# Sections of 12 tiles with one and two units of values in turn, and a last stretch of score pairs and whole products

## The chip, the cores and the metric

The kernel runs on one core of a Trainium2 chip. Its time is the device time of one execution in microseconds; the number compared is the median of several runs. Engines are named as in the profile: PE (TensorE), DVE (VectorE), ACT (ScalarE), POOL (GpSimd) and SP (the queue that issues most DMAs).

## What is computed

There are two branches over 2048 tokens of width 512, mixed by a gate for each token:

```python
a = x @ hid_re.T;  b = x @ hid_im.T            # 2048 x 512 each
y = seq_re @ a - seq_im @ b                    # a DFT of 2048 over the tokens, real part
q, k, v = split(xb @ wqkv)                     # 32 heads of 16
o = softmax(q @ k.T * 16**-0.5) @ v            # full attention, 2048 x 2048 for each head
g = sigmoid((x * gate_w).sum(-1))
out = g * y + (1 - g) * (o @ wo)
```

Everything is fp32. The weights of the attention are large, so the softmax needs each row's true maximum.

## The kernel before

**First stage** (to about 265 us of the span). The projections of x and xb are computed as sums of three products of high and low parts in fp32r (lines 78 to 80), and q and k go to DRAM.

**Main stage.** Two heads make a pair p, one in rows 0 to 63 of the array ("half 0"), one in rows 64 to 127 ("half 1"); products on different halves run at the same time. A pair has 32 *units* u: 2 halves of the queries (1024 each) by 16 blocks of 128 keys, so there are 512 units. Four kinds of work are interleaved:

- *a tile* (`a_tile`, line 196): a 128 x 512 block of scores in one of the three PSUM banks of `psA`, whose row maxima DVE takes (line 203). When 64 of them have closed half a pair, DVE reduces the maxima (`nm`, line 207), and `m_rows` (line 211) transposes them on PE into another `psA` bank, splits them on DVE and writes them by DMA into rows of `qs`, so that the scores come out with the maximum subtracted. The a tiles run 42 ahead of the units' need.
- *score* (`scores`, line 554), "s": keys by queries, 128 x 512, in one of the three banks of `psS`; ACT takes the exp into `pt` (line 564). A unit has four: two blocks of queries by two heads.
- *values* (`pv`, line 566): eight products of a unit on PE into the bank `acc`, in four column groups (line 572). After 16 units ACT copies `acc` out (line 576), and only then may the next unit write there.
- *DFT products* ("d", line 316): 32 chains of 48 products, each chain accumulating in the only bank of `psD`. Each product has 128 rows and is issued as two half products. A list of them is run first on half 0 while a tiles and scores run on half 1 beside it, then the same list on half 1 with tiles on half 0. Products on different halves may not write one bank together, so the first list product of a section waits for the reader (DVE or ACT) of a tile that was issued after the last one of the section before; line 726 adds that wait. At the end of a chain ACT or DVE reads the bank (lines 345, 348).

The order is written out by hand as patterns. Each token of a pattern is a slot: a single letter is one list product beside one tile on the other half; two letters are two tiles, one on each half, and no list product; a bar is one unit of values.

```python
FULL = "a s a s a s s a s a s a s a s a | |"
THIN = "aS s s a a s a | a s a a s s sA |"
```

FULL segments take lists of 16, and THIN segments lists of 12, so a chain takes three pairs of FULL or four pairs of THIN; the chains take turns (`pairs`, line 735). A segment holds two units. `pairs` goes on with eight THIN pairs over lists of 9 of the output product (`proj(1, (0, 1, 2))`), one chain for each list, read by DVE in `finish` (line 456).

**Last 30 units** (`weave`, line 613). Two units' scores with lists of 9 of the remaining output products, in half products, with a drain of PE ahead of each half (`turn`), then two units of values. Part of the scores use banks of `psA`. `last_pair` (line 494) turns the last sums by PE transposes, divides, multiplies by the last rows of wo and writes out.

**Plan.** `at(u, f)` runs a step ahead of unit u's section: `sums` loads the softmax sums from DRAM, `inverse` takes reciprocals on DVE (line 397), `block` and `last_block` load, multiply and split a block of the attention's output, and `load_yg` brings back the DFT result. `load_stacks` loads a pair's q and k.

Of the kernel before, what the change touches and what calls it, by code (L numbers as in the profile page):

```python
# [9 lines left out]
F32 = mybir.dt.float32  # L10
# [5 lines left out]
P = 128  # L16
S = 2048
D = 512
H = 32
DH = 16  # L20
NP = H // 2
KT = D // P
NT = S // P
UNITS = NP * 32
# [7 lines left out]
def mix_kernel(ctx: ExitStack, tc: tile.TileContext, xa_t, xa, wqkv, w_hid, w_seq, wo, gate_w, out):  # L32
# [5 lines left out]
    nc = tc.nc  # L38
# [142 lines left out]
    def load_stacks(p):  # L181
        q_t, k_t = qs[p % 2], ks[p % 2]
        for h in range(2):
            rows = slice((2 * p + h) * DH, (2 * p + h + 1) * DH)
            o = 64 * h

            for i, (qv, kv) in enumerate(((0, 0), (0, 1), (1, 0))):
                part = slice(o + 16 * i, o + 16 * i + 16)
                nc.sync.dma_start(q_t[part].bitcast(F32), qk_d[0][qv, rows])
                nc.sync.dma_start(k_t[part].bitcast(F32), qk_d[1][kv, rows])  # L190
# [33 lines left out]
    def run_deferred():  # L224
        while deferred:
            m_rows(*deferred.pop(0))
# [12 lines left out]
    a_next = 0  # L239
# [218 lines left out]
    def proj(hf, cts, pools):  # L458

        for qt in range(8):  # L460
            t = hf * 8 + qt
            chain = Chain(*pools[qt % len(pools)], 3 * len(cts))
            for ct in cts:
                h1, l1 = oh[hf, ct][qt]
                for i, (st, mv) in enumerate(((h1, 0), (h1, 1), (l1, 0))):
                    last = ct == cts[-1] and i == 2
                    yield chain, st, wos[0][:, mv, ct], partial(proj_next, hf, cts, t, chain) if last else None
# [6 lines left out]
    def load_yg(hf, ts):  # L474
        if hf:
            for t in ts:
                yp[t] = work.tile([P, D], F32, name=f"yp{t}", tag=("craw", "ch", "cl")[t % 3], bufs=3)
        else:
            for i, x in enumerate(("qs0", "ks0")):
                y4 = main.tile([P, 4, D], F32, name=f"yp_{x}", tag=x)  # L480
                yp.update({4 * i + k: y4[:, k] for k in range(4)})
        for t in ts:
            nc.sync.dma_start(yp[t], yg_d[t])

# [66 lines left out]

    pts = {}

    def scores(u, qb, h):
        p, r = divmod(u, 32)
        hf, kt = divmod(r, 16)
        q0 = hf * 1024 + qb * 512
        if u not in pts:
            pts[u] = work.tile([P, 4, 512], F32, name="pt", bufs=4)
        spare = a_next >= NP * 64 and qb and u < 500  # L560
        ps = psA.tile([P, 512], F32, name="a") if spare else psS.tile([P, 512], F32, name="s")
        rr = slice(64 * h, 64 * h + 50)
        nc.tensor.matmul(ps, ks[p % 2][rr, kt * P:(kt + 1) * P], qs[p % 2][rr, q0:q0 + 512], start=True, stop=True)  # L563
        return nc.scalar.activation(pts[u][:, 2 * qb + h], ps, AF.Exp, bias=0.0, scale=DH ** -0.5)  # L564
# [15 lines left out]
    def take(gen, n, whole=True):  # L580

        got = []
        while len(got) < n:
            x = next(gen, None)
            if x is None:
                break
            x[0].left -= 1
            got.append((*x, x[0].left == 0))
            if whole and got[-1][4]:
                break  # L590
        return got

    def issue(x, half, stop=True):
        chain, st, mv, after, last = x
        i = chain.mm(st, mv, half, last and stop)
        if stop and after:
            after()
        return i

    def turn():  # L600

        nc.tensor.drain()

    def pump(gen, n):
        for x in take(gen, n):
            issue(x, None)

    def drain(gen):
        while xs := take(gen, 9):
            for x in xs:  # L610
                issue(x, None)

    def weave(q, ds):

        m = len(q[0]) - 1
        n = min(len(ds), m)
        if ds:
            turn()
        for i in range(n):
            q[0][i]()  # L620
            issue(ds[i], 1, False)
        for x in ds[n:]:
            issue(x, 1, False)
        for i in range(n, m + 1):
            q[0][i]()
            q[1][i - n]()
        rest = q[1][m + 1 - n:]
        if ds:
            turn()
        for i, x in enumerate(ds):  # L630
            issue(x, 0)
            if i < len(rest):
                rest[i]()

    fill = iter(())
    plan = {2: [gate]}

    def at(u, f, *args):
        plan.setdefault(u, []).append(partial(f, *args))
# [9 lines left out]
                    for step, du in enumerate((16, 20, 22)):  # L649
                        at(last + du + 8 * half, block, step, hf, ct, half)  # L650

    def start(gen, n, whole=True):
        nonlocal fill, rate
        drain(fill)
        fill, rate = gen, (n, whole)

    one, more = [(psD, "d")], [(psD, "d"), (psA, "a"), (psA, "a")]
    at(482, start, proj(0, (0, 1, 2), one), 9)
    at(482, load_yg, 0, range(8))
    for step, u in enumerate((490, 494, 496)):  # L660
        at(u, last_block, step, 1, 3, nc.gpsimd)
    at(500, start, proj(1, (3,), more), 9, False)
    for step, u in enumerate((500, 502, 504)):
        at(u, last_block, step, 0, 4, nc.vector)
    at(506, start, proj(0, (3,), more), 9, False)
    at(500, load_w15)
    rate = (7, True)
    lead = a_next

    def ahead(k):  # L670
        return min(lead + 4 * k, NP * 64)

    def queue(k, h):

        q = []
        for i in range(4):
            q.append(partial(scores, 2 * k + i // 2, i % 2, h))
            if ahead(k) + i < NP * 64:
                q.append(partial(a_tile, ahead(k) + i, h))
        return q  # L680

    def run_plan(k):
        for f in plan.get(2 * k, []) + plan.get(2 * k + 1, []):
            f()
        if k % 16 == 0 and k // 16 + 1 < NP:
            load_stacks(k // 16 + 1)

    FULL = "a s a s a s s a s a s a s a s a | |"
    THIN = "aS s s a a s a | a s a a s s sA |"

    def stream(h):

        return (
            iter([(u, qb, h) for u in range(UNITS) for qb in range(2)]),
            iter([(i, h) for i in range(lead, NP * 64)]),  # L700
        )

    streams = [stream(h) for h in range(2)]

    def score(kind, h):
        x = next(streams[h][kind == "a"], None)
        if x:
            last_user[0] = (a_tile if kind == "a" else scores)(*x)

    last_user = [None]  # L710

    def segment(k, pattern, half, ds, stop):

        before = last_user[0]
        ds = iter(ds)
        u = 2 * k
        for slot in pattern.split():
            if slot == "|":
                pv(u)
                u += 1  # L720
                continue
            if len(slot) == 1:
                x = next(ds, None)
                i = x and issue(x, half, stop)
                if i and before is not None:
                    tc.add_manual_dep(
                        i.ins, before.ins.name,
                        mybir.DependencyInfo(mybir.DependencyClass.Sync, mybir.DependencyReason.DATA))
                    before = None
            score(slot[0], 1 - half)  # L730
            if len(slot) == 2:
                score(slot[1].lower(), half)
        run_deferred()

    def pairs():

        seq = dft()
        for i in range(2 * NT):
            for _ in range(4 if i % 2 else 3):
                yield THIN if i % 2 else FULL, take(seq, 12 if i % 2 else 16)  # L740
        seq = proj(1, (0, 1, 2), one)
        for i in range(8):
            yield THIN, take(seq, 9)

    run_plan(0)
    for i in range(4):
        for kind in "sa":
            for h in range(2):
                score(kind, h)
    pv(0)  # L750
    pv(1)
    for i in range(4):
        score("s", 0)
        score("a", 0)
    last_user[0] = None
    k = 1
    for pattern, ds in pairs():
        for half in range(2):
            run_plan(k)
            a_next = ahead(k)  # L760
            segment(k, pattern, half, ds, half == 1)
            k += 1
    for f in queue(k, 1):
        f()
    a_next = ahead(k + 1)
    for k in range(k, UNITS // 2):
        run_plan(k)
        if 2 * k in pts:
            continue
        q = [queue(k, 0), queue(k, 1)]  # L770
        a_next = ahead(k)
        weave(q, take(fill, *rate))
        pv(2 * k - 2)
        pv(2 * k - 1)
        run_deferred()
    pv(UNITS - 2)
    pv(UNITS - 1, evac=False)
    last_pair(fill)


# [34 lines left out]
```

## Time and profile before

| | us |
|---|---|
| median of 3 runs | 1836.16 |
| lowest, highest | 1835.36, 1836.42 |
| the profiled execution | 1838.79 |
| its span in the profile | 1837.0 |
| PE busy | 1803.5 |
| DVE busy | 1424.6 |
| ACT busy | 1164.2 |
| POOL busy | 306.5 |

The page gives each engine's busy time, a row of 40 slices of the span in tenths busy, the chain of work that ended last, and groups of instructions by line: tile written, tiles read, shapes, count, then busy time, mean length in ns, and idle time before with its releaser. A row of a timeline is start, length, engine, line, operation, tiles and count, with the idle time before it in brackets. Consecutive products on PE overlap in the records, so the distance of their starts is what they take. A row of the stretches gives the stretch, its length, the busy time and number of instructions of PE, PEld (weight loads), DVE, ACT and POOL, the granted PE clock, the DMA engines' share and GB/s.

### The profile page before, as it was taken

What the parts mean: (1) busy time and instruction counts of PE and PEld (TensorE: products, weight loads), DVE (VectorE), ACT (ScalarE), POOL (GpSimd) and SP (SyncE); (2) the same over time, 40 slices, a digit from 0 to 9 for tenths busy, and PEclk for the clock granted to TensorE, in tenths of its full rate; (3) what the DMA queues carried; (4) which work ended last, traced back from release to release, by engine and by line L of the source; (5) the groups of instructions that cost most, each with busy time, mean ns of one, the idle gap of its engine ahead of it and who ended that gap; (6) DMA issues with size and microseconds to landing.
All of it is one profiled execution on the core that took longest, in us unless ns stands there. A gap on an engine that the chain in (4) does not pass through costs nothing.

```text
span 1837.0 us, 32546 instructions
## 1 busy us (share of the span) xinstructions
PE 1803.5 (98%) x12672; PEld 1034.7 (56%) x12672; DVE 1424.6 (78%) x2375; ACT 1164.2 (63%) x2240; POOL 306.5 (17%) x317
## 2 busy tenths in 40 slices
PE   8999999999999999999999999999999999999998
PEld 7876665555555545555555555554655455544554
DVE  5236668888888888888888888888888888888824
ACT  5311126777777777767676677767676777777664
POOL 1210011111212123121112222221112221100000
PEclk9999989999999999999999999999999999999999
DMA  8783233131414153414271434223231524360212
GB/s 283 256 194 106 69 97 60 39 67 36 76 36 70 37 111 94 81 36 70 89 211 49 76 100 100 58 53 64 63 66 49 110 89 87 116 184 7 71 37 92
DMA packets 77994, 164.71 MB, mean 90 GB/s; under 512 B 14592, under 2 KB 15616, under 8 KB 74000
## 3 DMA queue, kind: packets, MB, share of 16 engines
q1 hardware_dynamic: 77584, 162.56, 35.1%
q8 instruction: 100, 1.64, 0.4%
q14 instruction: 54, 0.44, 0.1%
q0 software_dynamic: 256, 0.07, 0.0%
HBM read 107.47 MB, written 54.52 MB: 88 GB/s over the span
## 4 chain that ended last, share of the span: by engine, by line
PE 94%; DVE 4%; issue 1%; ACT 1%; DMA 0%; DVEq 0%; SPq 0%; ACTq 0%
PE d L316 34%; PE acc L572 26%; PE a L201 12%; PE s L563 8%; PE s L78 4%; PE s L79 3%; PE s L80 3%; DVE mx L203 2%; PE a L78 1%; PE a L79 1%; PE a L80 1%; PE a L316 1%; DVE yp L456 1%; DVE rc L397 0%; PE a L213 0%
## 5 line engine op out<-in xcount | busy, mean ns | idle before, releaser
L203 DVE TENSOR_REDUCE mx<-a 128x1 f32<-128x512 f32 x2048 | 1280.9, 683 | 261.3 <-PE a L201 208.9
L564 ACT ACTIVATE pt<-s 128x512 f32<-128x512 f32 x2032 | 1060.3, 612 | 447.2 <-PE s L563 385.3
L201 PE MATMUL a<-ks,qs 48*128 48x512 f32 x2048 | 809.8, 428 | 5.4 <-DVE mx L203 5.4
L563 PE MATMUL s<-qs,ks 50*128 50x512 f32 x2032 | 739.8, 418 | 3.7 <-DVE xab L75 1.8
L316 PE MATMUL d<-xab,ch 64*128 64x512 f32 x2048 | 671.5, 405 | 8.5 <-DVE mx L203 6.6
L572 PE MATMUL acc<-pt,vt 128*17 128x512 f32 x4096 | 537.6, 598 | 0.0
L316 PEld LDWEIGHTS d<-xab,ch 64*128 64x128 f32 x2048 | 358.4, 185 | 203.1 <-issue 118.1
L201 PEld LDWEIGHTS a<-ks,qs 48*128 48x128 f32 x2048 | 373.7, 186 | 160.4 <-DVE mx L203 120.9
L563 PEld LDWEIGHTS s<-qs,ks 50*128 50x128 f32 x2032 | 365.7, 186 | 73.9 <-ACT pt L564 35.2
L316 PE MATMUL d<-xab,cl 64*128 64x512 f32 x1024 | 406.0, 396 | 0.0
L295 POOL CAST ch<-craw 128x512 fp32r<-128x512 f32 x128 | 78.2, 611 | 1132.8 <-PE s L563 678.6
L316 PEld LDWEIGHTS d<-xab,cl 64*128 64x128 f32 x1024 | 189.1, 185 | 42.1 <-DVE mx L203 23.8
L572 PEld LDWEIGHTS acc<-pt,vt 128*17 128x17 f32 x4096 | 87.3, 96 | 198.4 <-issue 187.0
L296 POOL TENSOR_TENSOR cl<-craw,ch 128x512 fp32r<-128x512 f32 x128 | 164.1, 1282 | 10.2
L316 PE MATMUL d<-wo_hl,o_hl 64*128 64x512 f32 x288 | 78.7, 405 | 3.8 <-DVE mx L203 2.9
L78 PE MATMUL s<-wch,xab 128*128 128x512 f32 x192 | 79.9, 416 | 0.0
L80 PE MATMUL s<-wch,xab 128*128 128x512 f32 x192 | 76.0, 396 | 0.0
L79 PE MATMUL s<-wcl,xab 128*128 128x512 f32 x192 | 75.9, 395 | 0.0
L74 ACT CAST xab<-s 128x512 fp32r<-128x512 f32 x16 | 9.4, 585 | 97.6 <-PE s L79 97.6
L316 PEld LDWEIGHTS d<-wo_hl,o_hl 64*128 64x128 f32 x288 | 49.5, 184 | 30.2 <-issue 17.7
L78 PEld LDWEIGHTS s<-wch,xab 128*128 128x128 f32 x192 | 36.0, 188 | 16.1 <-issue 6.4
L75 DVE TENSOR_TENSOR hl<-s,hl 128x512 fp32r<-128x512 f32 x32 | 22.0, 686 | 27.1 <-ACT hl L74 27.1
(101 smaller groups left out, 693.3 us busy)
## 6 DMA issues: line engine op xcount, KB each, us to landing
craw<-w_seq SPq DMA_DIRECT2D x128, 256.0 KB
qk<-hl SPq DMA_DIRECT2D x32, 512.0 KB
qs<-qk SPq DMA_DIRECT2D x96, 128.0 KB
ks<-qk SPq DMA_DIRECT2D x96, 128.0 KB
b<-hl SPq DMA_DIRECT2D x16, 512.0 KB
xab<-b SPq DMA_DIRECT2D x16, 512.0 KB
o<-oe SPq DMA_DIRECT2D x62, 128.0 KB
oh<-nh SPq DMA_DIRECT2D x12, 512.0 KB
```

What stands on the lines that cost most here:

```text
L75: (lo_eng or nc.vector).tensor_tensor(lo, src, hi.bitcast(F32), ALU.subtract)
L78: nc.tensor.matmul(ps, sh, mh, start=first, stop=False)
L79: nc.tensor.matmul(ps, sh, ml, start=False, stop=False)
L80: nc.tensor.matmul(ps, sl, mh, start=False, stop=last)
L201: nc.tensor.matmul(ps, qs[p % 2][r, qt * P:(qt + 1) * P], ks[p % 2][r, kb * 512:(kb + 1) * 512], start=True, stop=True)
L203: user = nc.vector.tensor_reduce(mx[p % 2][:, h, qt, kb:kb + 1], ps, AX.X, ALU.max)
L295: nc.gpsimd.tensor_copy(h1, raw)
L296: nc.gpsimd.tensor_tensor(l1, raw, h1.bitcast(F32), ALU.subtract)
L316: i = nc.tensor.matmul(self.ps, st[r], mv[r], start=not self.begun, stop=stop)
L563: nc.tensor.matmul(ps, ks[p % 2][rr, kt * P:(kt + 1) * P], qs[p % 2][rr, q0:q0 + 512], start=True, stop=True)
L564: return nc.scalar.activation(pts[u][:, 2 * qb + h], ps, AF.Exp, bias=0.0, scale=DH ** -0.5)
L572: nc.tensor.matmul(acc[32 * j:32 * j + 17], vt[:, kt, p, 16 * h:16 * h + 17], pt[:, j], start=kt == 0, stop=kt == NT - 1)
```

## The change

One segment with two kinds of pattern becomes a section of 12 tiles, six of each kind for each pair and half. Values follow each section: one unit after the first section of a pair, two after the second, so a pair of sections has three units. Chains go in lists of 12 (every third chain) or of 10, 10, 10, 9 and 9; then come 13 lists of 9 of the output products, five more than before, which reach unit 491. `m_rows` runs after the first unit of values in a group. The wait of a section's first list product is on the last score's exp where there is a score among the tiles after the last list product, else on the first such tile. The last 20 units have no lists and no drains: both heads' scores go together, one in `psS` and one in `psA`, and some 128-row output products ("whole") come between the third and the fourth pair of them. Twelve whole products are left to `last_pair`. Some loads and steps of the plan are moved by a few units, and yg tiles 0 to 3 take other buffers.

```diff
+        elif ts[0] == 0:
+            for t, (tag, n) in zip(ts, (("ch", 3), ("yr", 1), ("y", 2), ("y", 2))):
+                yp[t] = work.tile([P, D], F32, name=f"yp{t}", tag=tag, bufs=n)
         else:
...
+            y4 = main.tile([P, 4, D], F32, name="yp_qs0", tag="qs0")
+            yp.update({t: y4[:, t - 4] for t in ts})
...
-    def scores(u, qb, h):
+    def scores(u, qb, h, other=False):
...
-        spare = a_next >= NP * 64 and qb and u < 500
-        ps = psA.tile([P, 512], F32, name="a") if spare else psS.tile([P, 512], F32, name="s")
+        ps = psA.tile([P, 512], F32, name="a") if other else psS.tile([P, 512], F32, name="s")
...
-    def turn():
-
-        nc.tensor.drain()
...
-    def weave(q, ds):
...
-    at(482, start, proj(0, (0, 1, 2), one), 9)
-    at(482, load_yg, 0, range(8))
-    for step, u in enumerate((490, 494, 496)):
+    at(462, load_yg, 0, range(4))
+    at(481, load_yg, 0, range(4, 8))
+    for step, u in enumerate((488, 492, 494)):
         at(u, last_block, step, 1, 3, nc.gpsimd)
-    at(500, start, proj(1, (3,), more), 9, False)
-    for step, u in enumerate((500, 502, 504)):
+    for step, u in enumerate((500, 504, 504)):
         at(u, last_block, step, 0, 4, nc.vector)
-    at(506, start, proj(0, (3,), more), 9, False)
-    at(500, load_w15)
...
+    at(498, load_w15)
...
-    FULL = "a s a s a s s a s a s a s a s a | |"
-    THIN = "aS s s a a s a | a s a a s s sA |"
+    SECTIONS = {
+        12: ("a s a s a s a s s a a s", "a s a s a s a s s a a s"),
+        10: ("a s a s s a a s s a aS", "aS a s s a s a s a s a"),
+        9: ("s a s a s a s a s aS", "a s a s a sS a a s aA s"),
+    }
...
+    def values(n):
+
+        nonlocal valued
+        for i in range(n):
+            pv(valued)
+            valued += 1
+            if i == 0:
+                run_deferred()
+
+    def section(pattern, half, ds):
+
+        nonlocal users
+        before = users
         ds = iter(ds)
...
             if len(slot) == 1:
-                x = next(ds, None)
-                i = x and issue(x, half, stop)
-                if i and before is not None:
+                i = issue(next(ds), half, half == 1)
+                users = []
+                if before:
                     tc.add_manual_dep(
-                        i.ins, before.ins.name,
+                        i.ins, dict(before).get("s", before[0][1]).ins.name,
...
         for i in range(2 * NT):
-            for _ in range(4 if i % 2 else 3):
-                yield THIN if i % 2 else FULL, take(seq, 12 if i % 2 else 16)
-        seq = proj(1, (0, 1, 2), one)
-        for i in range(8):
-            yield THIN, take(seq, 9)
+            for n in (12, 12, 12, 12) if i % 3 == 2 else (10, 10, 10, 9, 9):
+                yield take(seq, n)
+        for seq, n in ((proj(1, (0, 1, 2), one), 8), (first, 5)):
+            for i in range(n):
+                yield take(seq, 9)
...
-    for pattern, ds in pairs():
+    for ds in pairs():
         for half in range(2):
-            run_plan(k)
-            a_next = ahead(k)
-            segment(k, pattern, half, ds, half == 1)
-            k += 1
...
+            run_plan(valued + 1)
+            section(SECTIONS[len(ds)][half], half, ds)
+            values(half + 1)
+    for i in range(2):
+        score("s", 1)
...
+    whole = {492: (first, 9), 494: (first, 9), 496: (first, 9), 498: (third, 6), 500: (third, 6), 502: (third, 6),
+             504: (third, 6), 506: (last, 6), 508: (last, 3), 510: (last, 3)}
+    for u in range(valued + 1, UNITS, 2):
+        run_plan(u + 1)
+        for i in range(4):
+            if i == 3:
+                pump(*whole[u])
+            for h in range(2):
+                scores(u + i // 2, i % 2, h, h == 1)
+        while valued < u:
+            values(1)
     pv(UNITS - 2)
     pv(UNITS - 1, evac=False)
-    last_pair(fill)
+    last_pair(last)
```

More of the change, by code (lines that the diff above doesn't have):

```diff
@@ L477, in load_yg @@
                 yp[t] = work.tile([P, D], F32, name=f"yp{t}", tag=("craw", "ch", "cl")[t % 3], bufs=3)
-        else:
-            for i, x in enumerate(("qs0", "ks0")):
-                y4 = main.tile([P, 4, D], F32, name=f"yp_{x}", tag=x)
-                yp.update({4 * i + k: y4[:, k] for k in range(4)})
+        elif ts[0] == 0:
+            for t, (tag, n) in zip(ts, (("ch", 3), ("yr", 1), ("y", 2), ("y", 2))):
+                yp[t] = work.tile([P, D], F32, name=f"yp{t}", tag=tag, bufs=n)
+        else:
+            y4 = main.tile([P, 4, D], F32, name="yp_qs0", tag="qs0")
+            yp.update({t: y4[:, t - 4] for t in ts})
         for t in ts:
@@ L598, in issue @@
         return i
-    def turn():
-        nc.tensor.drain()
     def pump(gen, n):
-        for x in take(gen, n):
+        for x in take(gen, n, False):
             issue(x, None)
@@ L611, in drain @@
                 issue(x, None)
-    def weave(q, ds):
[L615 to L635, printed above, removed]
     plan = {2: [gate]}
@@ L650, in mix_kernel, with run_plan @@
                         at(last + du + 8 * half, block, step, hf, ct, half)
[L652 to L655, printed above, removed]
+    for p in range(1, NP):
+        at(32 * (p - 1) + 1, load_stacks, p)
     one, more = [(psD, "d")], [(psD, "d"), (psA, "a"), (psA, "a")]
-    at(482, start, proj(0, (0, 1, 2), one), 9)
-    at(482, load_yg, 0, range(8))
-    for step, u in enumerate((490, 494, 496)):
+    at(462, load_yg, 0, range(4))
+    at(481, load_yg, 0, range(4, 8))
+    for step, u in enumerate((488, 492, 494)):
         at(u, last_block, step, 1, 3, nc.gpsimd)
-    at(500, start, proj(1, (3,), more), 9, False)
-    for step, u in enumerate((500, 502, 504)):
+    for step, u in enumerate((500, 504, 504)):
         at(u, last_block, step, 0, 4, nc.vector)
-    at(506, start, proj(0, (3,), more), 9, False)
-    at(500, load_w15)
[L667 to L686, printed above, removed]
-    FULL = "a s a s a s s a s a s a s a s a | |"
-    THIN = "aS s s a a s a | a s a a s s sA |"
+    at(498, load_w15)
+    def run_plan(u):
+        for v in sorted(v for v in plan if v <= u):
+            for f in plan.pop(v):
+                f()
+    SECTIONS = {
[3 rows of a table added]
+    }
     def stream(h):
@@ L701, in stream @@
         )
+    lead = a_next
     streams = [stream(h) for h in range(2)]
+    valued, users = 0, []
     def score(kind, h):
@@ L707, in score @@
         if x:
[L708 to L714, printed above, removed]
+            users.append((kind, (a_tile if kind == "a" else scores)(*x)))
+    def values(n):
[8 more added lines that the diff above has]
+        before = users
         ds = iter(ds)
-        u = 2 * k
         for slot in pattern.split():
[L718 to L721, printed above, removed]
             if len(slot) == 1:
-                x = next(ds, None)
-                i = x and issue(x, half, stop)
-                if i and before is not None:
+                i = issue(next(ds), half, half == 1)
+                users = []
+                if before:
                     tc.add_manual_dep(
-                        i.ins, before.ins.name,
+                        i.ins, dict(before).get("s", before[0][1]).ins.name,
                         mybir.DependencyInfo(mybir.DependencyClass.Sync, mybir.DependencyReason.DATA))
@@ L732, in segment @@
                 score(slot[1].lower(), half)
-        run_deferred()
     def pairs():
@@ L738, in pairs @@
         for i in range(2 * NT):
-            for _ in range(4 if i % 2 else 3):
-                yield THIN if i % 2 else FULL, take(seq, 12 if i % 2 else 16)
-        seq = proj(1, (0, 1, 2), one)
-        for i in range(8):
-            yield THIN, take(seq, 9)
-    run_plan(0)
+            for n in (12, 12, 12, 12) if i % 3 == 2 else (10, 10, 10, 9, 9):
[3 more added lines that the diff above has]
+                yield take(seq, 9)
+    first = proj(0, (0, 1, 2), one)
     for i in range(4):
@@ L749, in mix_kernel @@
                 score(kind, h)
-    pv(0)
-    pv(1)
-    for i in range(4):
+    values(2)
+    for i in range(2):
         score("s", 0)
         score("a", 0)
-    last_user[0] = None
-    k = 1
-    for pattern, ds in pairs():
+    users = []
+    for ds in pairs():
         for half in range(2):
-            run_plan(k)
-            a_next = ahead(k)
-            segment(k, pattern, half, ds, half == 1)
-            k += 1
[L763 to L775, printed above, removed]
+            run_plan(valued + 1)
+            section(SECTIONS[len(ds)][half], half, ds)
+            values(half + 1)
+    for i in range(2):
+        score("s", 1)
+    third = proj(1, (3,), more)
+    last = proj(0, (3,), more)
+    whole = {492: (first, 9), 494: (first, 9), 496: (first, 9), 498: (third, 6), 500: (third, 6), 502: (third, 6),
[9 more added lines that the diff above has]
+            values(1)
     pv(UNITS - 2)
     pv(UNITS - 1, evac=False)
-    last_pair(fill)
+    last_pair(last)
 def kernel(A_x, A_dft_seq_re, A_dft_seq_im, A_dft_hid_re, A_dft_hid_im, B_x, B_wqkv, B_wo, gate_w):
```

## The prediction, made before the result was known

> **What bounds the kernel now.** I read the page first (slices, groups, chain), then the sums of four stretches, then the timelines of PE over single sections.
>
> ```profile
> PE   8999999999999999999999999999999999999998
> ...
> DVE  5236668888888888888888888888888888888824
> ...
> L203 DVE TENSOR_REDUCE mx<-a 128x1 f32<-128x512 f32 x2048 | 1280.9, 683 | 261.3 <-PE a L201 208.9
> L564 ACT ACTIVATE pt<-s 128x512 f32<-128x512 f32 x2032 | 1060.3, 612 | 447.2 <-PE s L563 385.3
> ```
>
> PE is busy in every slice and carries 94% of the chain, so the time is PE's issue, and what counts is where PE stops between products. Stretches: DFT, first output products, the woven rest, the end.
>
> ```profile
> 268.50:1624.80 1356.30, 1344.52 (x10282) 741.71 (x10278) 1154.66 (x1911) 960.38 (x1853) 269.72 (x277) 1.00 0.34 78
> 1624.80:1722.40 97.60, 94.67 (x663) 45.49 (x659) 86.79 (x143) 69.51 (x131) 1.84 (x2) 1.00 0.21 49
> 1722.40:1824.60 102.20, 97.87 (x633) 52.49 (x629) 43.31 (x67) 63.18 (x123) 4.92 (x3) 1.00 0.22 66
> 1824.60:1837.00 12.40, 7.10 (x32) 4.44 (x32) 7.99 (x24) 1.46 (x7) 0.00 (x0) 0.72 0.45 169
> ```
>
> The clock is 1.00 in the first three (column after POOL). DVE is busy 85 to 89% of the first two: little to spare. A FULL segment's end and the next one's start on PE:
>
> ```profile
> 704.50 0.39 PE L316 MATMUL d<-xab,ch 64*128 64x512 f32 x1
> 704.65 0.42 PE L201 MATMUL a<-ks,qs 48*128 48x512 f32 x1
> 705.00 1.91 PE L572 MATMUL acc<-pt,vt 128*17 128x512 f32 x16
> 706.84 0.50 PE L316 MATMUL d<-xab,ch 64*128 64x512 f32 x1
> ...
> 707.18 0.39 PE L563 MATMUL s<-qs,ks 50*128 50x512 f32 x1
> ```
>
> Read starts, not lengths. Products start every 0.23 to 0.25 us, the second of a section 0.34 after the first, values 0.35 after the last, and two units of values take 1.84. Over all sections 16 slots take 4.11, 7 slots 1.89 (so 0.247 a slot + 0.16), one unit 0.983, two 1.842. THIN:
>
> ```profile
> 311.94 0.40 PE L201 MATMUL a<-ks,qs 48*128 48x512 f32 x1
> 312.27 1.35 PE L572 MATMUL acc<-pt,vt 128*17 128x512 f32 x8
> 313.55 0.50 PE L316 MATMUL d<-xab,ch 64*128 64x512 f32 x1
> ...
> 315.40 1.05 PE L572 MATMUL acc<-pt,vt 128*17 128x512 f32 x8
> 316.39 0.50 PE L201 MATMUL a<-ks,qs 48*128 48x512 f32 x1
> ```
>
> The values in the middle of the first segment take 1.28, the others 0.98: they wait for the exp of a score issued five slots before. All 64 THIN pairs pay this 0.29. What a late DVE costs shows at 301 us:
>
> ```profile
> 299.95 3.07 DVE L203 TENSOR_REDUCE mx<-a 128x1 f32<-128x512 f32 x5
> ...
> 301.29 0.18 PEld L201 LDWEIGHTS a<-ks,qs 48*128 48x128 f32 x1 [0.24 <-DVE mx L203]
> ...
> 301.63 0.40 PE L563 MATMUL s<-qs,ks 50*128 50x512 f32 x1
> ...
> 301.88 0.18 PEld L201 LDWEIGHTS a<-ks,qs 48*128 48x128 f32 x1 [0.30 <-DVE mx L203]
> ```
>
> Five reductions in 3.07: one every 0.60, the last 0.68 long. A reduction starts 0.43 after its product (0.53 after a section's first), and its bank, one of three in psA, is free 0.05 after it ends. The product that waited is followed after 0.34, not 0.24. Exps likewise: one every 0.48, 0.61 long.
>
> **DFT, 450 units.** Three units hold 24 tiles and two passes over the list, so a pair of sections has 24, 22 or 21 slots, none half empty; before, a pair has 32 (FULL) or 28 (THIN) for four units. Slots per unit of work do not change. What goes: 352 groups of values become 300; each costs 0.28 (0.12 in its own time, 0.16 in its section): -15 us. The 0.29 of THIN, 18.5 us, goes: each unit's scores now lie a section earlier or in its early slots. At the end of the chains that THIN runs, the next chain's first product waits for bank d to be read (0.983 becomes up to 2.07, 9.6 us over medians); now two units of values, 1.84, lie over that 0.74 us read: gone. Without new waits a pair costs 2x3.12 + 0.98 + 1.84 = 9.07 (list of 12), 2x2.87 + 2.82 = 8.57 (10), 2.63 + 2.87 + 2.82 = 8.32 (9).
>
> New waits. (1) The second pattern for 9 has seven a tiles, in slots 1, 3, 5, 7, 8, 10 and 10 again. Reductions start at 0.53, 1.13, 1.73, 2.33; the seventh tile takes the bank of the fourth, free at 2.33 + 0.68 + 0.05 = 3.06. Its slot is due at 2.25. Behind it on PE stand slot 11 (+0.34) and the values (+0.35 to 0.44), and nothing passes them: 3.80, not 2.87, so the pair takes 9.25. The other patterns put six tiles in a section, and the sixth finds its bank with 0.05 to spare; a FULL segment's eighth had the same margin and gave it up only where another DVE step came in (+0.25). (2) The first list product of a section waits for an exp of the section before. In the middle of a pair one unit lies between. For 9: exps start 0.53, 1.01, ... 2.92, end 3.53, usable at 3.58; the product is due at 2.63 + 0.98 = 3.61. For 10 it is 3.84 against 3.85, and that second section opens with a slot that has no list product, 0.34 more. For 12 there is 0.25. All of PE stands behind that product if it waits. I take nothing, by a hair; the price without cover is a rival. (3) Units 15, 63, 111, ... 447, ten of them, end a half and come first in a group of two. The copy of acc starts 0.66 after the last product (all 31 copies do), takes 0.59, and the next unit follows 0.05 later; usual is 0.41: 0.89 each, 9 us. Least 0, if it hid, but it reads the bank that the next unit writes; most 1.0. (4) A transpose between two units costs 0.33 by its row (0.53 + 0.21 instead of 0.41), against 0.17 to 0.27 at a segment's start; reciprocals and m-row steps on DVE go on costing: I keep their 14 us of excess.
>
> Sum: 40x9.07 + 66x8.57 + 44x9.25 = 1335; + 14 + 9; + the start, 4.3 instead of 5.5 (four single slots fewer where they take 0.43): 1363. Before: 1356 for two units fewer (6 us). So the DFT gains nothing: wait 1 eats what the patterns save.
>
> **Output products in sections.** 13 lists of 9, 39 units: 13x9.25 = 120. The DVE finish of each chain (0.75) ends 0.1 before the next section's first product. Two single scores: 1.
>
> **Last 20 units.** Before, an iteration takes 7.0 (1753.66 to 1760.66): 18 half products, two drains; drain and turn cost 0.25 inside and 0.2 at the values. Now: three pairs at 0, 0.34, 0.58; nine wholes from 0.91 (0.33 after a pair, as in the first stage where 128-row and 48-row products meet), last at 2.86; fourth pair 3.19; values 3.62; end 5.46. With six 4.77, with three 4.07. Three with nine (the first of them has one unit of values, 0.86 less), five with six, two with three: 47.5; + 1.84 for the last two units, + 2.4 where a chain in psA waits for an exp to free its bank (units 500, 502, 508), + 2.3 at 504, where ACT's cast waits for the DVE product of the loaded block and all exps queue behind it: 54. Cover there: the loads took 9.35 from reciprocal to DVE, and I count 10. The steps moved on SP (yg loads at 462 and 481, the block at 488) lie behind landed work: POOL's product of that block ran 13.7 after its reciprocal, and now has 28 before ACT needs it. The end: 12 wholes and four finishes come into it; 0 if PE's idle 5.3 us hides them, 12x0.23 + 4x0.2 + 4x0.65 = 6.2 if nothing does; I take 3: 15.4.
>
> Wholes every 0.231 us is the spacing of the 128-row products at lines 78 to 80. The Trainium skill (TensorE: Matmul & The Clock Gate, The mechanism) says that a weight load overlaps products in flight "only when row_grp differs". The first stage, all 128 rows at 0.231, speaks against it; the last rival has its price.
>
> **Sum.** 268.5 + 1363 + 120 + 1 + 54 + 15.4 = 1822 against a span of 1837.0. The profiled execution took 1838.79, the median of three is 1836.16; so 1836 - 15 = 1821. About 0.2%, 3.7 us, is what can be told from no change.
>
> **Rivals.** *No seventh-tile wait*: the reductions keep up after all. 57 lists x 0.93 = 53 us: 1768. For it: DVE is only 87% busy over a pair. Against: the wait at 301 is this very one. 0.12. *Slower, the section start*: the one unit of values between the sections does not cover the exp. The common lag of an exp after its product is 0.68, not 0.43; if ACT comes 0.25 later, each list of 9 pays 0.25 + 0.1, and the others up to 0.05: 57x0.35 + 106x0.05 = 25, so 1846. It decides from 0.26 per list of 9. For it: margins of 0.03 and 0.01. Against: THIN's second segment starts on the same kind of wait, and its values still take 0.983. 0.18. *Loads of wholes exposed*: a whole waits for its own weight load, 0.188 by the loads of line 78, 75 wholes, +14 us: 1835, no change; against it the 0.231 above; 0.03. Forecast: 0.65, by itself 1806 to 1838 (the end 0 to 6, copies 0 to 10, DVE steps 8 to 25); 0.02 for none of these.
>
> Faster: 0.55 of the forecast and the first rival, 0.67. Same: 0.06 of the forecast, the loads' 0.03 and 0.03 of the slower rival and the rest, 0.12. Slower: 0.04 of the forecast, 0.16 of that rival, 0.01 of the rest, 0.21. The range leaves out half of the first rival and about 0.08 above.
>
> **What would show it.** In the profile after: values in groups of 0.98 and 1.84 with no 1.28; second sections of lists of 9 at 3.8 with a DVE wait at slot 10; ten groups of two at 2.7; last iterations near 5.5. Wrong if those sections take 2.9 (first rival), or if groups of one unit take 1.2 or more (second).

## The result, and the profile after

The changed kernel takes 1897.59 us (median of four runs) against 1836.16: 1.0337 times as long, 95% interval 1.0319 to 1.0355. The forecast was 1821, and the slowest time that the prediction worked out, that of its slower rival, was 1846. A gain was forecast, and it is a loss.

The page of the kernel after, slices and two groups:

```profile
PE   8999999999999999999999999999999999999998
...
DVE  5236567787788878777778878878878888878854
...
L203 DVE TENSOR_REDUCE mx<-a 128x1 f32<-128x512 f32 x2048 | 1273.0, 683 | 351.5 <-PE a L201 285.1
```

Nothing here shows 61 us: PE still reads 9 in every slice, since a slice is 47 us and "9" is 90% or more. The idle time before DVE's reductions is 351 us instead of 261, most of it ended by a tile's product on PE, so it is PE that is late. The stretches of the kernel after, with columns as in the ones before (DFT, output products in sections, the last 20 units, the end):

```profile
268.30:1706.40 1438.10, 1374.51 (x10308) 744.00 (x10304) 1155.96 (x1918) 964.17 (x1859) 269.70 (x277) 1.00 0.32 74
1706.40:1828.80 122.40, 120.88 (x865) 64.45 (x861) 106.18 (x178) 82.02 (x158) 4.22 (x3) 1.00 0.24 63
1828.80:1886.60 57.80, 54.08 (x329) 24.05 (x325) 16.38 (x24) 44.77 (x90) 2.54 (x2) 1.00 0.18 49
1886.60:1898.80 12.20, 7.05 (x32) 4.35 (x32) 8.70 (x25) 0.94 (x4) 0.00 (x0) 0.74 0.68 254
```

The DFT took 1438 us, and 1363 were forecast; the sections of output products 122 (120). From 1828.8 to the end of the last values, 1883.85, it is 55.1 (1 + 54), and from there to the end 15.0 (15.4). So 75 of the 77 us by which the forecast missed lie in the DFT. Most of it is PE idle time: 64 us of 1438, against 12 of 1356 before. The waits of PE's weight loads in the main stage name the releaser:

```profile
PEld d L316 <- ACT pt L565: 148.1, 156, 1.2
PEld a L201 <- DVE mx L203: 133.3, 314, 1.9
```

List products wait for an exp 156 times; before, that row was not among the leading ones. (A load that stands behind values counts 0.85 us as idle here without harm, so only the rest of each wait is lost.) Taken apart by pattern, medians of 40 to 66 sections each, from the start of a section to the start of its values, and from there to the next section:

| | section, then values | forecast | measured |
|---|---|---|---|
| list of 12 | first; second | 3.12 + 0.98; 3.12 + 1.84 | 3.17 + 0.98; 3.18 + 1.84 |
| list of 10 | first; second | 2.87 + 0.98; 2.87 + 1.84 | 2.92 + 0.98; **3.81** + 1.84 |
| list of 9 | first; second | 2.63 + 0.98; 3.80 + 1.84 | 2.61 + 1.04; 3.77 + 1.84 |

One entry is far off. This is the start of such a section in the kernel after, PE, PE's loads and ACT in one timeline:

```profile
725.53 1.05 PE L573 MATMUL acc<-pt,vt 128*17 128x512 f32 x8
726.51 0.50 PE L201 MATMUL a<-ks,qs 48*128 48x512 f32 x1
726.52 0.49 PE L564 MATMUL s<-qs,ks 50*128 50x512 f32 x1
...
727.13 0.60 ACT L565 ACTIVATE pt<-s 128x512 f32<-128x512 f32 x1
727.79 0.18 PEld L316 LDWEIGHTS d<-xab,ch 64*128 64x128 f32 x1 [1.09 <-ACT pt L565]
727.79 0.50 PE L316 MATMUL d<-xab,ch 64*128 64x512 f32 x1 [0.78 <-ACT pt L565]
...
728.13 0.40 PE L564 MATMUL s<-qs,ks 50*128 50x512 f32 x1
```

The first list product starts 1.28 after the section's first slot instead of 0.34, and 0.06 after the end of an exp that itself began in this section. That exp reads the score of slot 1, the capital S of "aS". The product waits for a tile issued just ahead of it.

The code says why. `before = users` gives the list of the last section's tiles a second name, it doesn't copy it. The first slot of "aS a s s ..." calls `score` twice before any list product, and `score` appends to that same list. So when the first list product looks for the last "s" in `before`, it finds the score of its own section. Where a section opens with a list product, nothing has been appended yet, and the wait is the one meant.

### The profile page after: what moved, and what is told of

Its sections match the earlier page's. It is cut to its first block, busy times and chain, and to the rows that moved or that the text cites. A ratio compares the mean times of both kernels' runs of the same rounds, so it can differ in the third digit from the quotient of the medians.

```text
span 1898.8 us, 32351 instructions
## 1 busy us (share of the span) xinstructions
PE 1816.0 (96%) x12597; PEld 1027.6 (54%) x12597; DVE 1419.1 (75%) x2375; ACT 1162.0 (61%) x2240; POOL 306.2 (16%) x317
## 4 chain that ended last, share of the span: by engine, by line
PE 85%; DVE 10%; ACT 3%; issue 1%; DMA 1%; SPq 0%; DVEq 0%; ACTq 0%
PE d L316 34%; PE acc L573 25%; DVE mx L203 9%; PE a L201 8%; PE s L564 6%; PE s L78 4%; PE s L79 3%; PE s L80 3%; ACT pt L565 2%; PE a L78 1%; PE a L79 1%; PE a L80 1%; ACT oe L577 0%; PE a L213 0%; DMA o_raw<-r 0%
## 5 line engine op out<-in xcount | busy, mean ns | idle before, releaser
L565 ACT ACTIVATE pt<-s 128x512 f32<-128x512 f32 x2008 | 1044.7, 605 | 503.6 <-PE s L564 456.0
L201 PE MATMUL a<-ks,qs 48*128 48x512 f32 x2048 | 835.8, 433 | 10.8 <-DVE mx L203 4.3
L564 PE MATMUL s<-qs,ks 50*128 50x512 f32 x2008 | 768.1, 419 | 2.0 <-DVE xab L75 1.7
L573 PE MATMUL acc<-pt,vt 128*17 128x512 f32 x4096 | 513.9, 599 | 7.1 <-ACT oe L577 7.1
L564 PEld LDWEIGHTS s<-qs,ks 50*128 50x128 f32 x2008 | 372.6, 186 | 33.2 <-ACT pt L565 15.4
L573 PEld LDWEIGHTS acc<-pt,vt 128*17 128x17 f32 x4096 | 83.1, 96 | 216.7 <-issue 197.4
L316 PE MATMUL d<-wo_hl,o_hl 64*128 64x512 f32 (+1 forms) x261 | 72.2, 402 | 0.1
L316 PEld LDWEIGHTS d<-wo_hl,o_hl 64*128 64x128 f32 (+1 forms) x261 | 46.1, 185 | 26.8 <-issue 12.3
```

The costliest lines, as they stand in the source:

```text
L201: nc.tensor.matmul(ps, qs[p % 2][r, qt * P:(qt + 1) * P], ks[p % 2][r, kb * 512:(kb + 1) * 512], start=True, stop=True)
L316: i = nc.tensor.matmul(self.ps, st[r], mv[r], start=not self.begun, stop=stop)
L573: nc.tensor.matmul(acc[32 * j:32 * j + 17], vt[:, kt, p, 16 * h:16 * h + 17], pt[:, j], start=kt == 0, stop=kt == NT - 1)
```

## The experiments

**1. The list copied.**

```diff
-        before = users
+        before = list(users)
```

> The changed kernel with one edit: a section keeps a copy of the list of the last section's tiles, so that the tiles of its own first slot don't enter the choice of the exp that its first list product waits for. Theory (self-wait): in the second section of a list of 10, whose first slot holds two tiles and no list product, the wait falls on the exp of the section's own score, 0.53 + 0.61 + 0.05 after it, where 0.34 is due; without it that section goes from 3.81 to 2.9 us, 66 times 0.9 = 60 us, and the kernel to 1836 +- 6. Rival (late release: an exp of the section before comes too late for the short cover of one unit of values): the section stays at 3.8 and the kernel at 1890 to 1898, since the wait is on the older exp in either case.

Measured: 1837.69 us, 1.0003 of the kernel before (0.9994 to 1.0012). The second section of a list of 10 fell from 3.81 to 2.90, the others didn't move. The same stretch in this run:

```profile
705.16 1.05 PE L573 MATMUL acc<-pt,vt 128*17 128x512 f32 x8
...
706.14 0.49 PE L201 MATMUL a<-ks,qs 48*128 48x512 f32 x1
706.15 0.49 PE L564 MATMUL s<-qs,ks 50*128 50x512 f32 x1
...
706.48 0.39 PE L316 MATMUL d<-xab,ch 64*128 64x512 f32 x1
```

The list product follows after 0.34. The row of waits, over the same window, has lost exactly the 66 sections:

```profile
PEld d L316 <- ACT pt L565: 79.7, 90, 0.9
```

148.1 - 79.7 = 68 us of waiting gone, 60 us of time. The late-release rival expected 1890 or more, so it is out.

**2. The pattern turned, the list not copied.**

```diff
-        10: ("a s a s s a a s s a aS", "aS a s s a s a s a s a"),
+        10: ("a s a s s a a s s a aS", "a s a s s a s a s a aS"),
```

> The changed kernel with the second pattern for lists of 10 turned, so that it opens with a list product and ends with the slot of two tiles; nothing else. Theory (self-wait): the opener is what makes the wait fall on its own score, so the section falls to 2.9 to 3.1 as with the copied list; the last score's exp is now needed by the values behind it (0.1 us each): 1836 to 1846. Rival (late release): the first list product now comes 0.34 us earlier after the values and waits 0.3 us longer: 1895 to 1915.

Measured: 1845.95 (1.0046, 1.0031 to 1.0061). The section takes 2.94 and the values after it 1.90, 0.06 more: in the trace one product of their second unit now starts 0.05 after the end of the exp of the section's last slot. So the opener of two tiles is what turns the shared list into a wait. The margin of 0.01 us that I had computed for this case, a list of 10 whose second section opens with a list product, held: the values before it stay at 0.983.

**3. Six a tiles in each section of a list of 9,** on top of the copied list. (As the change was written, the two sections of a list of 9 hold 11 and 13 tiles, five and seven of them a tiles, and not 12.)

```diff
-        9: ("s a s a s a s a s aS", "a s a s a sS a a s aA s"),
+        9: ("a s a s s a s a s aA", "aS s a s a s a s a s sA"),
```

> The copied list, and lists of 9 with six a tiles in each section instead of five and seven. Theory (the seventh tile waits for DVE to free the bank of the fourth): the second section of a list of 9 falls from 3.77 to about 3.0, the first rises from 2.61 to about 2.85; 57 lists times 0.55 = 31 us under the copied list alone, 1805 +- 8. Rival (the section is long for another reason, its two slots without list products or the exps): no more than 5 us under the copied list.

Measured: 1815.35 (0.9881, 0.9866 to 0.9895), 22 us under the copied list: less than the 31 expected, and 2 us outside its band, but far beyond the rival's 5. The second section went from 3.77 to 3.12, the first from 2.61 to 2.93. What the seventh tile did is seen in the kernel after; a section begins at 974.09, and these are its DVE row and its last slots:

```profile
974.66 3.68 DVE L203 TENSOR_REDUCE mx<-a 128x1 f32<-128x512 f32 x6 [0.36 <-PE a L201]
...
976.01 0.50 PE L201 MATMUL a<-ks,qs 48*128 48x512 f32 x1
...
976.60 0.18 PEld L201 LDWEIGHTS a<-ks,qs 48*128 48x128 f32 x1 [0.30 <-DVE mx L203]
976.60 1.09 PE L201 MATMUL a<-ks,qs 48*128 48x512 f32 x2
977.20 0.18 PEld L201 LDWEIGHTS a<-ks,qs 48*128 48x128 f32 x1 [0.42 <-DVE mx L203]
...
977.85 0.62 PE L573 MATMUL acc<-pt,vt 128*17 128x512 f32 x4
```

The tiles come at DVE's pace of 0.60, the seventh at 977.20, 3.11 after the start where I had 3.06. In the even section the seventh score is what waits now, for ACT:

```profile
937.99 0.18 PEld L564 LDWEIGHTS s<-qs,ks 50*128 50x128 f32 x1 [0.31 <-ACT pt L565]
938.00 0.49 PE L201 MATMUL a<-ks,qs 48*128 48x512 f32 x1
...
938.42 0.13 PEld L573 LDWEIGHTS acc<-pt,vt 128*17 128x17 f32 x8 [0.24 <-issue]
```

That score starts at 937.99, 2.69 after the section's start (935.30), where I had 2.63. The sections take 3.12 and 2.93 where I expected 3.0 and 2.85: 57 times 0.2 is 11 us less gain. The values between the two sections went from 1.04 to 0.98, which gives 3 us back, so it is 22 and not 31.

**4. The self-wait put into the kernel before.**

```diff
                 i = x and issue(x, half, stop)
+                before = before and last_user[0]
                 if i and before is not None:
```

> The kernel before with the self-wait put in: the first list product of a segment waits for the last tile issued, so in THIN segments for the exp of the score in their own first slot. Theory: 144 THIN segments open with two tiles and pay 0.9 each, less 0.5 in eight where bank d is late anyway: 125 us, 1955 to 1965. Rival (late release is what costs, not the self-wait): under 30 us, below 1866.

Measured: 1953.95 (1.0631, 1.0613 to 1.0649), 117 us more, where the rival allowed 30. A THIN segment of this run:

```profile
330.74 0.50 PE L201 MATMUL a<-ks,qs 48*128 48x512 f32 x1
330.75 0.50 PE L563 MATMUL s<-qs,ks 50*128 50x512 f32 x1
331.31 0.60 ACT L564 ACTIVATE pt<-s 128x512 f32<-128x512 f32 x1 [0.36 <-PE s L563]
331.96 0.18 PEld L316 LDWEIGHTS d<-xab,ch 64*128 64x128 f32 x1 [1.03 <-ACT pt L564]
```

The list product comes 1.22 after the opener, not 0.34. The 144 sections that open with two tiles grew by 131 us, 0.91 each, as expected. 14 us came back, because the values behind them no longer wait for an exp: in the kernel before 63 such groups take over 1.2, in this run none. What remains is 117.

**5. The copy of acc kept from between two units,** on top of 3.

```diff
+    behind = 0
...
-            run_plan(valued + 1)
+            run_plan(valued + behind + 1)
...
-            values(half + 1)
+            n = valued + half + 1 + behind
+            behind = int(half == 1 and valued % 16 == 15)
+            values(n - valued - behind)
```

> The kernel with even lists of 9 (and the copied list), and where the first of two units of values ends a half (ten times) the second one is put off to the next group, so that no unit follows the copy of acc at once. Theory (that copy holds PE for 0.89 each time): the groups of 2.6 to 2.7 us become 0.98, the next one 1.84, and the kernel gains 6 to 9 us: 1806 to 1810. Rival (the wait only moves: the next section's first list product, now after one unit, waits instead): 0 to 3 us, 1812 to 1816.

Measured: 1808.47 (0.9849, 0.9836 to 0.9863), 6.9 us less than experiment 3. In the kernel after, PE, one of the ten:

```profile
472.47 1.05 PE L573 MATMUL acc<-pt,vt 128*17 128x512 f32 x8
474.23 0.62 PE L573 MATMUL acc<-pt,vt 128*17 128x512 f32 x4 [0.71 <-ACT oe L577]
```

The second unit starts 1.76 after the first; usual is 0.86.

**6. The transposes after the whole group,** on top of 5: `run_deferred()` moves out of the loop in `values`.

> As the last one, and the transposes of the row maxima run after the whole group of values instead of after its first unit. Theory (a transpose between two units costs 0.33, ahead of a section 0.19): some 20 times 0.14, 2 to 4 us under the last one, 1803 to 1807. Rival (later transposes hold the two DVE steps and the next section's a tiles): the same as the last one or 2 us more.

Measured: 1808.33 (0.9845, 0.9832 to 0.9859), the same as 5. The 2 to 4 us didn't come, and the traces of the two runs show why. The groups of two units with a transpose became shorter: 2.05 instead of 2.17, and three that had taken 2.6 to 3.4 came down with them, 4.2 us in all. But the sections right behind the transposes became longer by 4.4 us. Four of them account for that: three that had their usual length in 5 take 1.2 more, and a fourth goes from 0.6 to 1.2 over the usual. In the one at 685.7, DVE's two steps behind the transpose and two reciprocals (1.11 us) come first, and its first reduction of a tile starts only at 687.48. So the rival was right: the later transposes hold the next section's a tiles.

**7. Drains back around the whole products,** on top of 5: `nc.tensor.drain()` ahead of and behind `pump` in the last ten iterations.

> The kernel with the copied list, even lists of 9 and the copy of acc alone, and a drain of PE ahead of and behind the whole products of each of the last ten iterations; nothing else. Theory (a drain costs on top of the turn from 64 to 128 rows, 0.2 to 0.25 each as in the woven iterations of the kernel before): 20 drains, 4 to 5 us more, 1812 to 1814, and the distance from the third pair of scores to the first whole product goes from 0.32 to about 0.5. Rival (PE empties anyway where the tiling changes): 0 to 1 us, 1808 to 1810.

Measured: 1810.91 (0.9859, 0.9842 to 0.9875), 2.4 us more than 5, between the two theories and not told from it by the intervals. The trace does tell. Third pair of scores, wholes and fourth pair, with drains and (second fence, the run of 5) without:

```profile
1748.54 0.39 PE L564 MATMUL s<-qs,ks 50*128 50x512 f32 x1
...
1749.08 2.33 PE L316 MATMUL d<-wo_hl,o_hl 128*128 128x512 f32 x9
1751.51 0.49 PE L564 MATMUL s<-qs,ks 50*128 50x512 f32 x1
```

```profile
1748.55 0.39 PE L564 MATMUL s<-qs,ks 50*128 50x512 f32 x1
...
1748.87 2.33 PE L316 MATMUL d<-wo_hl,o_hl 128*128 128x512 f32 x9
1751.13 0.50 PE L564 MATMUL s<-qs,ks 50*128 50x512 f32 x1
```

0.54 against 0.32 ahead of the wholes, and 2.43 against 2.26 from there to the fourth pair: in an iteration that waits for nothing else, a drain costs about 0.2 on top of the turn. The sum of 4 to 5 us that I built on this didn't come. From the first whole to the first whole of `last_pair`, all ten iterations, the traces have 53.9 us with drains and 52.9 without. Four iterations are 0.35 to 0.37 longer, five change by less, most of them with waits of their own, and the one of unit 504 is 0.97 shorter, because its pause of 1.40 between the third and the fourth whole has become the usual 0.23.

## Why the prediction was wrong, point by point

**The step that failed** is the second of the new waits, where it treats lists of 10: "that second section opens with a slot that has no list product, 0.34 more". I read that opener as 0.34 us more of cover for an exp of the section before. It is what lets the section's own score into the list that the wait is chosen from, and the product then waits 0.94 more. Experiment 1 takes that away alone and gives back 60 of the 61 us of loss (of the 77 us between forecast and result); experiment 4 makes the same loss, 0.91 for each such section, in the other kernel. The sentence of the change's section that puts the wait on the tiles of the section before is true only of sections that open with a list product. The fault was in reading the code, not in a duration. None of the signs that the prediction named could have shown it: values of 0.98 and 1.84, second sections of lists of 9 at 3.8, ten groups of two at 2.7 and last iterations near 5.5 all came, and no sign was set on second sections of lists of 10.

**The slower rival** had the sign, and the first list product of a section waiting for an exp, but another exp and other lists: the last exp of the section before, 0.25 late, mostly at lists of 9. That wait exists. Groups of one unit there take 1.04 instead of 0.98, and the next section starts 0.05 after the end of an exp. But it costs 0.06 for each of 57 lists, 3 us in all and not 25.

**What stood.** The seventh tile: 3.80 forecast, 3.77 measured, and the rival without that wait is out (experiment 3). The copy of acc: 0.89 forecast, 0.90 measured. The wait of THIN's values is gone: past the start, no group of one unit without a transpose takes more than 1.05 (with one, 1.19). So is the late bank: the group of two at a chain's end takes 1.84 to 1.89 in 22 of 32 chains. Of the other ten, five hold a transpose and two the copy of acc; the last three take 2.00, 2.02 and 2.94, which I had not foreseen. The last 20 units: 55 forecast, 55.1 measured. The sum is closer than its terms: the waits for a bank at units 500, 502 and 508 took 2.5 (2.4), but the wait at 504 took 1.3 where 2.3 was forecast, and small waits between wholes that I had left out filled most of the gap. An iteration of nine wholes took 5.42 us (1839.99 to 1845.41) where I had 5.46:

```profile
1839.99 0.49 PE L564 MATMUL s<-qs,ks 50*128 50x512 f32 x1
...
1840.88 2.33 PE L316 MATMUL d<-wo_hl,o_hl 128*128 128x512 f32 x9
1843.14 0.50 PE L564 MATMUL s<-qs,ks 50*128 50x512 f32 x1
1843.14 0.49 PE L564 MATMUL a<-qs,ks 50*128 50x512 f32 x1
1843.57 1.91 PE L573 MATMUL acc<-pt,vt 128*17 128x512 f32 x16
1845.41 0.50 PE L564 MATMUL s<-qs,ks 50*128 50x512 f32 x1
```

From the first of nine wholes to the fourth pair it is 2.26, 0.23 from product to product after the first two, so the loads of 128 rows are hidden, and the rival with exposed loads is out.

**What was too small.** With the list copied the DFT still takes 1377 us, not 1363: a pair of a list of 12 takes 9.17 instead of 9.07, one of 10 takes 8.64 instead of 8.57 (8 us), and the excess over the medians is 5 us larger than the 23 allowed. So against 1356 for two units fewer, the sections as written lose some 14 us beside the self-wait. What lies behind the DFT wins about as much (192 us against 212 before, with two units fewer), and with the list copied the two kernels come out equal.

The version of experiment 5 beats both: 1808.47, 1.5% under the kernel before.

## What to carry to other kernels

When a schedule is written in a program, a wait is what the program builds, not what its names say: look in the trace for the releaser of the first product of a section, and ask whether that instruction started before or inside the section. A releaser that started inside it is a dependence on work the waiter stands beside. Where two engines' queues fill from short patterns, count tiles per section against banks and the reader's pace (here three banks, 0.60 a read): an average of 87% says nothing about a section that holds seven.

## What the runs showed of the hardware

Going from the pairs of 64-row products to a 128-row product and back cost time both ways: the first whole starts 0.32 after the pair, where 0.23 is usual, and the second whole 0.34 after the first; the pair behind the wholes starts 0.32 after the last one. A drain instruction at the turn cost 0.2 more (0.54 against 0.32 ahead of the wholes, 2.43 against 2.26 behind them) in an iteration that waits for nothing else. The Trainium skill (TensorEngine Tiling (Array Packing), Key Properties) says that changing the tiling mode drains TensorE, so I had to expect that a drain placed there might be free. In that iteration it is not: the trace shows both costs, one on top of the other.
